# First chunk of a sparse-attention and MoE kernel: copies of the transposed exponentials ahead of the put-off weight operations

## The chip, the cores and the metric

The kernel runs on one core of one Trainium2 chip. The metric is the device time of one execution in microseconds (us); the time before is the median of three runs. A core has a matrix engine (TensorE, PE in the rows, its weight loads PEld), a vector engine (VectorE, DVE), a scalar engine (ScalarE, ACT), GpSimd (POOL) and SyncE (SP). Each engine takes its instructions in the order in which they are written for it, and they wait for each other by semaphores. DMAs are issued from the queues of SyncE, ScalarE and GpSimd; in the rows ACTq is ScalarE's queue where it issues one.

## What is computed

Block-sparse attention over 4 batches, 8 heads, 768 positions and 64 dimensions a head, and then a two-layer network with a gate on its output, cut here to what matters:

```python
scores = scale * np.matmul(q, k.transpose(0, 1, 3, 2))
scores = np.where(mask, scores, -1000000000.0)   # blocks of 32: the diagonal and its neighbours, the edges, 3 drawn ones a row
attn = np.exp(scores - np.max(scores, axis=-1, keepdims=True))
attn = attn / (np.sum(attn, axis=-1, keepdims=True) + 1e-09)
x = np.matmul(attn, v)                            # then laid out as 3072 tokens x 512
h = x @ w_in                                      # 512 -> 2048
g = h * (1.0 / (1.0 + np.exp(-1.702 * h)))
out = g @ w_out                                   # 2048 -> 512
```

## The kernel before

The tokens are worked in six chunks of 512. A chunk of the network has 16 steps (m, 0 to 15 in the first chunk), one for each slice of 128 of the inner dimension. In step m TensorE does twelve up-projection matmuls of slice m (L565 to L567, `up`) and twelve down-projection matmuls of slice m - 1 (L616, L617, L612, `down`). Each matrix is held as a high and a low part (`xhi`, `xlo`; the two halves of `win` and `wout`; `ghi`, `glo`), and each product is the sum of three of these matmuls. Between the two, ScalarE takes a tanh of the up-projection's bank (L573, `gate`), in steps before 13 also copies the bank to `wst` so that it comes free (L578), VectorE makes the gate (L580), ScalarE its high part (L585) and VectorE its low part (L593).

The attention of the next chunk runs between these matmuls, one item in two steps, by a plan that `plan` makes ahead of time. At the start of an even step TensorE computes an item's scores (L323) into banks 0 and 1 and, behind them, the values of the item before (L401) into bank 2. VectorE takes the rows' maximum (L340, L342) and normalises the item before (L417 to L427), and ScalarE does the exponentials (L354). At the start of the odd step behind it TensorE transposes the exponentials into banks 0 and 1 (L372) and the finished x of the item before into bank 2 (L434). ScalarE copies the two banks to `pt` (L378, two copies), and then makes x's high part (L441, `xhi`), from which VectorE makes the low part (L442, `xlo`). The next item's scores need banks 0 and 1 again, so they wait for the copies; the values need `pt` and bank 2, so they wait for the copies and for L442.

In the first chunk alone, `weights` also turns the 32 weight tiles from 64-bit words to two parts. A tile k is fetched by a DMA of 512 KB on ScalarE's queue (L467, `raw`). ScalarE takes the high word (L477, `a`), VectorE works three operations on it (L515, L517, L526), ScalarE casts the high part (L492) and, for a `wout` tile, issues its store to DRAM (L494, `ws`), and VectorE makes the low part (L485). Up-projection m needs `win` tile m, down-projection m needs `wout` tile m. `run(n0)`, `run(n1)` and `run(n2)` in `tick` let this generator take some steps. What it does on VectorE is written at once. What it does on ScalarE (the DMAs too) is put into the list `self.late`, and `self.flush()` writes the whole list. So the places where `tick` calls `flush` set where the weight operations stand among ScalarE's other instructions.

In `tick`, a step's first calls are the low part of the gate before (VectorE), `flush`, and `begin`, which writes what the plan has for the step's start. `begin` writes the matmuls at once and returns the rest in `after`: in an odd step the two copies and the pair L441 and L442, in an even step the maximum, the exponentials and the normalisation. `finish(after[:4])` writes them.

Of the kernel before, what the change touches and what calls it, by code (L numbers as in the profile page):

```python
# [39 lines left out]
QT = 4  # L40
# [14 lines left out]
class Kernel:  # L55
# [646 lines left out]
    def tick(self, m):  # L702

        n0, n1, n2 = 0, 0, 0
        if m < NF:
            heavy = any(part == self.scores for q in range(QT) for part, g in self.at.get(QT * m + q, ()))
            n0, n1, n2 = (2, 2, 4) if heavy else (2, 2, 2)

        def run(n):
            for _ in range(n):  # L710
                next(self.conv, None)

        def finish(todo):
            for f in todo:
                f()

        self.gate_lo(m - 1)
        self.flush()
        after = self.begin(QT * m)
        finish(after[:4])  # L720
        run(n0)
        finish(after[4:])
        self.up(m, range(0, 2))
        self.put_off = []
        finish(self.begin(QT * m + 1))
        put_off, self.put_off = self.put_off, None
        self.up(m, range(2, 4))
        after = self.begin(QT * m + 2)
        self.gate(m, lambda: (self.flush(), run(n1)))
        finish(put_off)  # L730
        finish(after[:3])
        self.down(m - LAG, 0)
        self.gate_hi(m)
        self.flush()
        finish(after[3:])
        finish(self.begin(QT * m + 3))
        self.down(m - LAG, 1)
        self.split(m + 1)
        self.stream(m + 3)
        run(n2)  # L740
# [315 lines left out]
```

## Time and profile before

| | |
|---|---|
| three runs, us | 744.56, 746.95, 746.97; median 746.95 |
| profiled execution, us | 741.64 |
| its span, us | 739.9 |
| busy, us (share of the span) | TensorE 719.3 (97%), weight loads 564.2 (76%), VectorE 449.8 (61%), ScalarE 388.4 (52%), GpSimd 63.3 (9%) |
| granted TensorE clock | 0.997 over the span |
| DMA | 122.97 MB, 166 GB/s over the span |

The shares of busy time are means over stages with different limits: the attention of the first units runs alone until about 75 us, the first chunk with the weights' conversion until about 197 us, and the other chunks behind it. A busy TensorE counts a matmul from its start to a modelled end, also where matmuls of one group wait for each other's banks. What a stage is worth is read from a table of stretches and from the timeline of that stage. In the table, steps are cut at the first up-projection matmul (L565) of each, so that a step's piece begins with its up-projection and ends with what the plan sets at the start of the step behind it: an even step's with the transposes, an odd step's with scores and values.

### The profile page before, as it was taken

What the parts mean: (1) busy time and instruction counts of PE and PEld (TensorE: products, weight loads), DVE (VectorE), ACT (ScalarE), POOL (GpSimd) and SP (SyncE); (2) the same over time, 40 slices, a digit from 0 to 9 for tenths busy, and PEclk for the clock granted to TensorE, in tenths of its full rate; (3) what the DMA queues carried; (4) which work ended last, traced back from release to release, by engine and by line L of the source; (5) the groups of instructions that cost most, each with busy time, mean ns of one, the idle gap of its engine ahead of it and who ended that gap; (6) DMA issues with size and microseconds to landing.
All of it is one profiled execution on the core that took longest, in us unless ns stands there. A gap on an engine that the chain in (4) does not pass through costs nothing.

```text
span 739.9 us, 18756 instructions
## 1 busy us (share of the span) xinstructions
PE 719.3 (97%) x7564; PEld 564.2 (76%) x7564; DVE 449.8 (61%) x839; ACT 388.4 (52%) x759; POOL 63.3 (9%) x105
## 2 busy tenths in 40 slices
PE   8899999998999999999999999999999999999996
PEld 5666777776777787777877787778878788888885
DVE  4595888788654445455444544554567877676552
ACT  4686666656554454445444454544334554445442
POOL 2245101011011111100111111100000000000000
PEclk9999999999999999999999999999999999999998
DMA  8997877768476576657565555631111301110532
GB/s 325 363 363 250 282 251 249 244 195 285 170 225 198 154 206 197 189 156 229 185 188 175 164 180 168 194 114 31 43 43 43 86 29 43 30 42 30 143 113 71
DMA packets 58776, 122.97 MB, mean 166 GB/s; under 512 B 7105, under 2 KB 24898, under 8 KB 58690
## 3 DMA queue, kind: packets, MB, share of 16 engines
q1 hardware_dynamic: 44978, 76.72, 34.0%
q0 software_dynamic: 6336, 23.43, 9.7%
q10 hardware_dynamic: 7376, 21.63, 8.6%
q8 instruction: 59, 0.97, 0.5%
q14 instruction: 27, 0.22, 0.1%
HBM read 111.26 MB, written 10.49 MB: 165 GB/s over the span
## 4 chain that ended last, share of the span: by engine, by line
PE 74%; DVE 11%; DMA 7%; ACT 5%; issue 2%; SPq 1%; ACTq 0%; POOL 0%; DVEq 0%
PE banks L612 10%; PE banks L616 10%; PE banks L617 9%; PE banks L825 9%; PE banks L565 6%; PE banks L566 5%; PE banks L567 5%; PE banks L401 5%; PE banks L372 5%; PE banks L323 5%; DMA raw<-in_moe_w_in_dram 2%; DMA vmid<-in_v_dram 2%; PE banks L333 1%; DVE g L580 1%; DVE a L517 1%
## 5 line engine op out<-in xcount | busy, mean ns | idle before, releaser
L616 PE MATMUL banks<-wout,ghi 128*128 128x512 f32 x384 | 151.5, 395 | 0.0
L617 PE MATMUL banks<-wout,ghi 128*128 128x512 f32 x384 | 149.9, 390 | 1.3 <-DVE wout L485 1.3
L354 ACT ACTIVATE ex<-banks,nm 128x256 f32<-128x256 f32 x176 | 69.0, 478 | 77.9 <-DVE rg L417 66.0
L612 PE MATMUL banks<-wout,glo 128*128 128x512 f32 x384 | 107.6, 394 | 1.2 <-DVE glo L593 1.2
L565 PE MATMUL banks<-xhi,win 128*128 128x512 f32 x256 | 105.0, 410 | 1.5 <-DVE g L580 1.1
L566 PE MATMUL banks<-xlo,win 128*128 128x512 f32 x256 | 100.3, 392 | 0.0
L567 PE MATMUL banks<-xhi,win 128*128 128x512 f32 x256 | 100.1, 391 | 0.0
L554 DVE TENSOR_TENSOR wout<-wst,wout 128x512 fp32r<-128x512 f32 x80 | 55.2, 690 | 68.6 <-ACT wout L553 68.0
L617 PEld LDWEIGHTS banks<-wout,ghi 128*128 128x128 f32 x384 | 72.2, 188 | 16.6 <-DVE wout L485 2.1
L616 PEld LDWEIGHTS banks<-wout,ghi 128*128 128x128 f32 x384 | 72.1, 188 | 15.9 <-ACT ghi L585 0.5
L573 ACT ACTIVATE g<-banks 128x512 f32<-128x512 f32 x64 | 38.5, 602 | 86.7 <-PE banks L567 86.7
L612 PEld LDWEIGHTS banks<-wout,glo 128*128 128x128 f32 x384 | 70.7, 188 | 17.3 <-DVE glo L593 2.8
L378 ACT COPY pt<-banks 128x512 f32<-128x512 f32 x112 | 60.9, 588 | 29.4 <-PE banks L372 27.0
L265 POOL DMA_INDIRECT vown<-in_v_dram,vidx x44 | 42.7, 970 | 380.2 <-PE banks L401 367.9
L585 ACT CAST ghi<-g 128x512 fp32r<-128x512 f32 x80 | 50.1, 626 | 45.4 <-DVE g L580 37.6
L580 DVE SCALAR_TENSOR_TENSOR g<-g,banks 128x512 f32<-128x512 f32 x51 | 35.0, 687 | 59.1 <-ACT g L573 58.7
L340 DVE TENSOR_REDUCE mx<-banks 128x4 f32<-128x1024 f32 x44 | 53.7, 1221 | 26.5 <-PE banks L323 24.5
L372 PEld LDWEIGHTS banks<-ident,ex 128*128 128x128 f32 x448 | 50.4, 140 | 18.1 <-ACT pt L378 6.7
L372 PE MATMUL banks<-ident,ex 128*128 128x128 f32 x448 | 61.0, 276 | 3.1 <-ACT pt L378 2.8
L565 PEld LDWEIGHTS banks<-xhi,win 128*128 128x128 f32 x256 | 48.1, 188 | 13.8 <-ACT wst L578 1.8
L401 PEld LDWEIGHTS banks<-vown,pt 128*32 128x32 f32 x1408 | 42.3, 109 | 18.4 <-issue 13.8
L567 PEld LDWEIGHTS banks<-xhi,win 128*128 128x128 f32 x256 | 48.1, 188 | 10.5
(111 smaller groups left out, 1098.9 us busy)
## 6 DMA issues: line engine op xcount, KB each, us to landing
wst<-ws SPq DMA_DIRECT2D x80, 256.0 KB, 2.7
kg<-in_kb_dram SPq DMA_DIRECT2D x126, 128.0 KB, 3.0
raw<-in_moe_w_in_dram ACTq DMA_DIRECT2D x16, 512.0 KB, 5.6
raw<-in_moe_w_out_dram ACTq DMA_DIRECT2D x16, 512.0 KB, 5.7
kg<-in_kb_dram SPq DMA_DIRECT2D x18, 384.0 KB, 5.3
vown<-in_vd_dram SPq DMA_DIRECT2D x8, 780.0 KB
vmid<-in_v_dram SPq DMA_DIRECT2D x22, 260.0 KB, 4.0
qt<-in_q_dram SPq DMA_DIRECT2D x22, 256.0 KB, 3.1
```

Of the source, the lines that this page charges most:

```text
L354: nc.scalar.activation(out=ex[:, cols], in_=sps[h][:, cols], func=AF.Exp, bias=un["nm"][:, c:c + 1], scale=SCALE)
L372: self.nc.tensor.transpose(ps[:, slot], g["ex"][h][:, k * P:(k + 1) * P], self.ident)
L378: self.nc.scalar.copy(out=pt, in_=ps)
L401: nc.tensor.matmul(sums[BLK * c:BLK * (c + 1), 2 * i + h], g["pt"][h][:, 2 * i + k, BLK * c:BLK * (c + 1)], src[:, at:at + DV], start=(k = ...
L554: self.nc.vector.tensor_tensor(out=t[:, DM:2 * DM], in0=w, in1=t[:, 0:DM].bitcast(F32), op=ALU.subtract)
L565: nc.tensor.matmul(h, wih[:, k], hi[:, k], start=(k == 0), stop=False)
L566: nc.tensor.matmul(h, wih[:, k], lo[:, k], start=False, stop=False)
L567: nc.tensor.matmul(h, wil[:, k], hi[:, k], start=False, stop=(k == NCT - 1))
L612: nc.tensor.matmul(o[n], glo[:, tk[n]], woh, start=False, stop=last)
L616: nc.tensor.matmul(o[n], ghi[:, tk[n]], woh, start=(f == 0), stop=False)
L617: nc.tensor.matmul(o[n], ghi[:, tk[n]], wol, start=False, stop=False)
L825: self.nc.tensor.matmul(bank, a[:, k], b[:, k], start=start and k + n == 0, stop=k == 1 and n == 2, skip_group_check=True)
```

## The change

```diff
--- before.py
+++ after.py
@@ -714,10 +714,13 @@
             for f in todo:
                 f()
 
+        turning = any(part == self.transposes for part, g in self.at.get(QT * m, ()))
         self.gate_lo(m - 1)
-        self.flush()
+        if not turning:
+            self.flush()
         after = self.begin(QT * m)
         finish(after[:4])
+        self.flush()
         run(n0)
         finish(after[4:])
         self.up(m, range(0, 2))
```

In a step whose plan begins with transposes, the first `flush` is left out, and the list is written behind `finish(after[:4])`. In the other steps the first `flush` stands as it did, and the second finds the list empty, since `begin` puts nothing into it. From step 16 on the list is always empty. The steps with transposes at their start and something in the list are 1, 3, 5, ... 15: eight places, all on ScalarE.

This is the piece of the order on ScalarE at the start of step 11 (`pt` takes the copies of the transposed exponentials; `a`, `raw` and `win` belong to the weight tiles; the tanh L573 is step 11's own):

```order
 L467 DMA raw<-in_moe_w_in_dram 128x1024
 L477 ACTIVATE a<-raw 128x512
+L378 COPY pt_130<-banks 128x512
+L378 COPY pt_131<-banks 128x512
+L441 CAST xhi_125<-banks 128x4x64
 L492 CAST win_1959<-a 128x512
 L467 DMA raw<-in_moe_w_out_dram 128x1024
 L477 ACTIVATE a<-raw 128x512
-L378 COPY pt_130<-banks 128x512
-L378 COPY pt_131<-banks 128x512
-L441 CAST xhi_125<-banks 128x4x64
 L573 ACTIVATE g<-banks 128x512
```

The copies and the cast of x have moved ahead of a weight cast, the issue of a transfer and an L477.

The same on ScalarE at the start of step 13:

```order
 L492 CAST wout_120<-a 128x512
 L494 DMA ws_95<-a 128x512
+L378 COPY pt_129<-banks 128x512
+L378 COPY pt_130<-banks 128x512
+L441 CAST xhi_125<-banks 128x4x64
 L467 DMA raw<-in_moe_w_in_dram 128x1024
 L477 ACTIVATE a<-raw 128x512
 L492 CAST win_1961<-a 128x512
-L378 COPY pt_129<-banks 128x512
-L378 COPY pt_130<-banks 128x512
-L441 CAST xhi_125<-banks 128x4x64
```

Here the three have moved ahead of the issue of a transfer, an L477 and a weight cast. The order of the three among themselves, and that of the weight operations among themselves, is as it was.

## Rows read from the trace of the kernel before

**Rows 1.** The page's chain of waits: shares of the span by engine.
```profile
PE 74%; DVE 11%; DMA 7%; ACT 5%; issue 2%; SPq 1%; ACTq 0%; POOL 0%; DVEq 0%
```

**Rows 2.** Stretches: A:B, length, busy us (instructions) of PE, PEld, DVE, ACT, POOL; clock, DMA.
```profile
87.17:196.92 109.75, 105.59 (x1084) 80.32 (x1079) 90.76 (x171) 69.97 (x138) 8.75 (x8) 1.00 0.72 235
196.92:739.87 542.95, 534.53 (x5146) 427.39 (x5140) 301.14 (x534) 260.54 (x513) 26.21 (x28) 1.00 0.43 128
```

**Rows 3.** Stretches: odd steps 3, 5, 7, 9, 11, and the sum of all seven.
```profile
93.75:102.05 8.30, 8.28 (x124) 5.99 (x122) 5.42 (x11) 5.08 (x11) 0.00 (x0) 1.00 0.52 165
109.34:117.09 7.75, 7.75 (x120) 5.87 (x120) 6.16 (x12) 5.77 (x11) 0.00 (x0) 1.00 0.80 259
123.91:132.52 8.61, 8.33 (x122) 6.01 (x121) 5.67 (x11) 5.32 (x11) 0.00 (x0) 1.00 0.58 189
139.82:148.14 8.32, 8.32 (x120) 6.22 (x120) 5.73 (x11) 5.67 (x11) 0.00 (x0) 1.00 0.88 270
155.37:164.53 9.16, 8.30 (x121) 6.01 (x121) 5.67 (x11) 5.33 (x11) 0.00 (x0) 1.00 0.46 153
...
sum 59.07, PE 56.82 PEld 41.73 DVE 41.51 ACT 37.02 POOL 0.92; mean PE 8.12 PEld 5.96 DVE 5.93 ACT 5.29 POOL 0.13
```

**Rows 4.** Stretches: even steps 2, 12, 14, and the sum of all seven.
```profile
87.17:93.75 6.58, 6.58 (x40) 5.57 (x35) 6.41 (x15) 4.54 (x10) 2.59 (x2) 1.00 0.85 296
...
164.53:171.83 7.30, 7.14 (x41) 5.48 (x35) 7.13 (x15) 4.87 (x11) 0.00 (x0) 1.00 0.97 298
180.75:188.91 8.16, 6.89 (x35) 5.50 (x35) 7.75 (x15) 5.22 (x11) 1.09 (x2) 1.00 0.87 292
sum 50.68, PE 48.77 PEld 38.59 DVE 49.24 ACT 32.95 POOL 7.83; mean PE 6.97 PEld 5.51 DVE 7.03 ACT 4.71 POOL 1.12
```

**Rows 5.** Waits, 87.17 to 196.92 us: us in total, times, longest.
```profile
DVE xlo L442 <- ACT xhi L441: 14.3, 6, 3.4
...
PE banks L617 <- DVE wout L485: 1.3, 1, 1.3
...
PE banks L565 <- DVE g L580: 1.1, 1, 1.1
```

**Rows 6.** ScalarE by line, the same stretch: count | busy, mean | idle before.
```profile
L477 ACT ACTIVATE a<-raw 128x512 f32<-128x512 f32 x23 | 15.7, 682 | 10.7 <-DMA raw<-in_moe_w_in_dram 7.1 <-DMA raw<-in_moe_w_out_dram 3.6
```

**Rows 7.** Timeline, ScalarE, step 11: start us, us, what, idle before.
```profile
156.85 0.68 ACT L477 ACTIVATE a<-raw 128x512 f32<-128x512 f32 x1
157.53 0.62 ACT L492 CAST win<-a 128x512 fp32r<-128x512 f32 x1
...
160.78 0.66 ACT L477 ACTIVATE a<-raw 128x512 f32<-128x512 f32 x1 [2.63 <-DMA raw<-in_moe_w_in_dram]
161.35 1.06 ACT L378 COPY pt<-banks 128x512 f32<-128x512 f32 x2
162.29 0.39 ACT L441 CAST xhi<-banks 128x256 fp32r<-128x256 f32 x1
```

**Rows 8.** Timeline, VectorE, steps 11 and 12.
```profile
158.64 0.69 DVE L593 TENSOR_TENSOR glo<-g,ghi 128x512 fp32r<-128x512 f32 x1
162.71 0.42 DVE L442 TENSOR_TENSOR xlo<-banks,xhi 128x256 fp32r<-128x256 f32 x1 [3.38 <-ACT xhi L441]
...
164.25 0.42 DVE L515 TENSOR_SCALAR a<-a 128x512 int32<-128x512 int32 x1
...
167.72 1.22 DVE L340 TENSOR_REDUCE mx<-banks 128x4 f32<-128x1024 f32 x1
```

**Rows 9.** Timeline, TensorE: scores at the start of step 12.
```profile
161.97 1.58 PE L323 MATMUL banks<-kg,qt 64*32 64x256 f32 x32 [0.86 <-ACT pt L378]
```

**Rows 10.** Timeline, ScalarE and its queue (ACTq), steps 13 and 14.
```profile
175.35 0.33 ACTq L467 DMA_DIRECT2D raw<-in_moe_w_out_dram  x1
175.52 0.61 ACT L492 CAST win<-a 128x512 fp32r<-128x512 f32 x1
...
178.48 0.72 ACT L477 ACTIVATE a<-raw 128x512 f32<-128x512 f32 x1 [0.61 <-DMA raw<-in_moe_w_in_dram]
```

## The prediction

> **What bounds the kernel now.** I read the chain of waits first. Over the whole run TensorE carries most of it, with VectorE, DMA and ScalarE behind [rows 1], so the first question is where those three have their shares. The table of stretches answers it: behind 196.92 us TensorE is busy 534.53 of 542.95 us, while the 109.75 us from 87.17 to 196.92 (steps 2 to 15 of the first chunk) leave it 4.16 us without work, and its busy time there also counts matmuls stretched by waits inside them [rows 2]. The change touches steps 1 to 15 alone, so this stretch is the place to look.
>
> Next I cut the stretch at the first up-projection matmul of each step. An odd step's piece, with the next item's scores and values at its end, lasts 7.75 us at best (step 5) and 9.16 at worst (step 11) [rows 3]. An even step's, with the transposes at its end, lasts 6.58 us at best (step 2), 8.16 at worst (step 14) and 50.68 together [rows 4]. The matmuls are the same in all steps of a kind, so I take the shortest as what TensorE needs. The excess is then: odd steps 3, 7, 9, 11: 0.55 + 0.86 + 0.57 + 1.41 = 3.39 us; odd steps 13 and 15 share the rest of the odd steps' 59.07 us: 59.07 - 7 x 7.75 - 3.39 = 1.43; even steps 50.68 - 7 x 6.58 = 4.62, of which step 14 has 8.16 - 6.58 = 1.58 and steps 4 to 12 share 3.04. Together 9.44 us of 109.75. That is all the change can win here.
>
> Then I asked the list of waits who makes them. VectorE idles 14.3 us, in six odd steps, until ScalarE's cast L441 releases the subtraction L442; two single waits of TensorE, 1.1 us for L580 and 1.3 us for L485, stand in step 14 [rows 5]. ScalarE in its turn idles 10.7 us before L477, all of it for weight transfers [rows 6]. So the order on ScalarE is late, that makes VectorE late, and that makes TensorE late.
>
> **The change, part by part.** Nothing is added or removed. On ScalarE alone, in eight steps (1, 3, ... 15), two copies of transposed exponentials (L378) and one cast of x (L441) go ahead of two to four put-off weight instructions. TensorE, VectorE, GpSimd and SyncE keep their orders.
>
> Step 11 in full. ScalarE runs L477 at 156.85, then the cast L492 at 157.53, then a second L477 that waits 2.63 us for its transfer until 160.78, and only then the two copies at 161.35 and the cast of x at 162.29 [rows 7]. The transposes were done before the step's first up-projection matmul at 155.37 [rows 3], so nothing but the order holds the copies back. After the change they take the place of L492: two copies from 157.53 to 158.6 (1.06) and the cast to 158.9 (it starts 0.94 after the copies and takes 0.39). L492 and the second L477 follow, and L477 is still free well before its transfer lands at 160.78.
> - VectorE: L442 came at 162.71, after 3.38 us of idling behind L593 at 158.64 [rows 8]. Now it can start at about 159.3. The next instruction that needs ScalarE's late work is L515, which reads what L477 leaves at 160.78 + 0.66 = 161.44; it ran at 164.25, so VectorE is 2.8 us ahead from there, and keeps a wait of about half a microsecond, for the transfer.
> - TensorE: the scores L323 started after 0.86 us of waiting for the copies, and took 1.58 us because the second copy came while they ran [rows 9]. With the copies done at 158.6 both go, and with x's subtraction done at 159.7 the values that write its bank do not wait either. The step falls to 7.75: 1.41 us.
> - The even step behind it: the maximum L340 ran at 167.72 [rows 8]. Its inputs are there earlier, so it moves by VectorE's 2.8 us while TensorE moves by 1.41. The exponentials then lead the transposes by 1.4 us more than before, and this covers step 12's 7.30 - 6.58 = 0.72 us.
>
> The sum over the steps:
> - Odd steps 3, 7, 9, 11: I carry step 11 over to the other three, where three or four weight instructions move in the same way. 3.39 us go, nothing stays.
> - Even steps 4 to 12: 3.04 us. VectorE's six idle stretches of 14.3 us shrink to the waits for transfers, which were 10.7 us of ScalarE's idling [rows 6] and now lie beside 7 x 1.33 = 9.3 us of copies and casts. I leave 0.3 us.
> - Steps 13 to 15: 1.43 + 1.58 = 3.01 us. Up-projection 14 starts after 1.1 us of waiting for L580, which is behind L442 on VectorE, and goes. The 1.3 us at L617 are for the weight half L485, which stands on VectorE behind step 14's maximum and normalisation, whose start TensorE itself sets. I leave 1.0 us.
> Gain 9.44 - 0.3 - 1.0 = 8.1, taken as 8.0 us.
>
> What it could cost: seven of the moved groups hold a weight transfer (L467), and its issue is now behind three more instructions. A transfer has no row in this place, so I bound it. At the top, its issue slips by the whole copies and cast, 1.33 us. At the bottom, nothing: in step 13 the transfer of the step after is issued at 175.35, while the weight cast, two copies, cast of x and tanh that stand ahead of it all start later, from 175.52 on [rows 10]; the queue passes them as soon as what they wait for is there. I take 0.2 us, nearer to that row. It hides wherever the reader comes late: step 11's is read one L477 behind the one that still waits at 160.78. Step 13's is read without slack (L477 at 178.48 waits 0.61 us for it [rows 10]); it stays inside the 1.0 us left above. The Trainium skill, page DMA: Bandwidth & Descriptors, section Rules for kernel authors, says to issue a DMA early, compute, and wait for it late, and so speaks against setting three instructions before each issue. By that rule a slip of 1.33 us would be paid at seven issues; the row of step 13 shows the issue passing such instructions, so the trace does not agree that it is paid here.
>
> VectorE does not become the bound: it has 90.76 us of work [rows 2] for the 100.3 us (7 x 14.33) that TensorE needs. The gain lasts, since TensorE is 98% busy behind 196.92 and starts all of it earlier.
>
> The profiled execution took 741.64 us (739.9 of span and 1.7 around it); the sum would bring it to 733.6. The three timed runs (744.56 to 746.97) lie above it, and nothing in the profile says where; I take the 8.0 us off their median: 746.95 - 8.0 = 739.0.
>
> **The rivals.**
> - Direct waits alone go. If VectorE, freed from L442, stands as long at L515 or L485 for ScalarE's moved weight operations, the exponentials come no earlier, and only the 3.39 us of the scores' waits are won: 743.6. For it: L515 and L485 both read ScalarE's results. Against it: in step 11 the moved L477 ends when its transfer lets it, in either order.
> - Transfers become the bound. With everything else earlier, L477 waits longer; 10.7 us of it [rows 6] are there already. Were half of the 3.04 and all but 0.5 of the 3.01 us to stay, the gain is 3.39 + 1.52 + 0.5 = 5.4: 741.5. For it: the DMA engines are busy 72% of the stretch [rows 2]. Against it: the issues hang on the same steps, so they come earlier too.
> - Slower: the weight chain is delayed. If the weight operations behind the copies, their transfers included, are what VectorE and then TensorE wait for last, each of seven steps adds 1.33 us, 9.3 in all, less the 3.39: 5.9 us slower, 752.9. It decides from the point where the transfer's issue really slips by the copies and its reader has no slack; the trace shows that slack missing in step 13 alone. The Trainium skill's rule on early issue, in DMA: Bandwidth & Descriptors, Rules for kernel authors, would lead here.
> - No change: the steps get shorter, but the lead is lost to a wait behind 196.92, for instance on stored weights read back; 746.95. Against it stands TensorE's 98% there.
>
> **How the numbers follow.** A measurement of this kernel tells about 0.5%, 3.7 us, from no change. Forecast (gain 5.6 to 9.4): 0.60. Transfers: 0.17. Direct waits alone: 0.13. No change 0.05, slower 0.05. The range takes in the forecast, the transfers and the direct waits: from 735.2 (the whole 9.44 us off the middle of the runs and their spread) to 743.8. The forecast's own range is 737.5 to 741.3. Faster: 0.60 + 0.17 + nearly half of 0.13 = 0.83. Within 0.5%: 0.12. Slower: 0.05.
>
> **What would show it.** The stretch between the first up-projection matmuls of steps 2 and 16 falls from 109.75 to about 101.6 us, odd steps near 7.75 and even ones near 6.6. L442's waits for L441 fall from 14.3 us to under 4; ScalarE's waits for transfers stay or grow; no scores wait for L378; at L617 a wait for L485 may stay. I am wrong if VectorE's idling only changes its place to L515 or L485, if even steps keep 7.3 us, or if step 13 or 14 waits longer for a weight tile than before.

## The result and the profile after

The change took the median from 745.75 us (four runs of the kernel before, 743.33 to 746.97) to 734.75 (four runs, 733.50 to 735.92): a ratio of 0.9856, interval 0.9822 to 0.989. The forecast was 739.0 and its range began at 735.2, so the time lies 0.45 us below the range. The profiled execution took 734.98 us, with a span of 733.2.

In all tables below, the stretch runs from the first up-projection matmul of step 2 to that of step 16, and "opening" is what lies before step 0's. The columns of the next fences are those of [rows 2]. First the two stretches of the kernel after:

```profile
89.32:190.24 100.92, 100.40 (x1085) 79.85 (x1079) 89.04 (x168) 68.89 (x137) 7.49 (x8) 1.00 0.79 256
190.24:733.20 542.96, 534.49 (x5146) 427.29 (x5140) 301.21 (x534) 260.76 (x513) 26.22 (x28) 1.00 0.43 128
```

The stretch fell from 109.75 us [rows 2] to 100.92, by 8.83, and all behind it stayed at 542.96: the gain lasts. The chain of waits, which had VectorE at 11% and ScalarE at 5 [rows 1], by engine after:

```profile
PE 82%; DMA 7%; DVE 6%; ACT 3%; issue 1%; ACTq 0%; DVEq 0%
```

TensorE gained the shares that the two lost. The odd step 11 and the sum of the seven odd steps, after:

```profile
153.10:160.82 7.72, 7.72 (x124) 5.85 (x122) 4.83 (x9) 3.89 (x9) 0.00 (x0) 1.00 0.56 218
...
sum 54.04, PE 54.04 PEld 40.96 DVE 44.88 ACT 35.98 POOL 0.00; mean PE 7.72 PEld 5.85 DVE 6.41 ACT 5.14 POOL 0.00
```

The even steps 12 and 14, after:

```profile
160.82:167.40 6.58, 6.58 (x40) 5.56 (x35) 6.33 (x13) 4.52 (x10) 0.00 (x0) 1.00 0.90 277
175.12:182.52 7.40, 6.88 (x40) 5.49 (x35) 7.16 (x15) 5.03 (x11) 1.87 (x2) 1.00 0.96 296
```

All seven odd steps take 7.72 us and six of the seven even ones 6.58; the scatter of [rows 3, 4] is gone but for step 14, 0.82 us above the others. ScalarE and VectorE by line in the stretch, after (columns as in [rows 6]):

```profile
L477 ACT ACTIVATE a<-raw 128x512 f32<-128x512 f32 x23 | 15.6, 678 | 15.7 <-DMA raw<-in_moe_w_in_dram 9.0 <-DMA raw<-in_moe_w_out_dram 4.2 <-DMA kg<-in_kb_dram 1.4
L515 DVE TENSOR_SCALAR a<-a 128x512 int32<-128x512 int32 x23 | 9.8, 424 | 7.9 <-ACT a L477 7.6
...
L442 DVE TENSOR_TENSOR xlo<-banks,xhi 128x256 fp32r<-128x256 f32 x7 | 2.9, 419 | 0.0
```

VectorE's 14.3 us of idling before L442 [rows 5] are gone. The idling moved to two places where TensorE doesn't feel it: before L515 on VectorE, and before L477 on ScalarE, which idles 5.0 us longer than before [rows 6]; the view puts 13.2 of these 15.7 us down to weight transfers, and all 10.7 before. Step 11 shows how. ScalarE and its queue, after (columns as in [rows 7]):

```profile
151.46 0.33 ACTq L467 DMA_DIRECT2D raw<-in_moe_w_in_dram  x1
151.93 0.69 ACT L477 ACTIVATE a<-raw 128x512 f32<-128x512 f32 x1
152.73 1.08 ACT L378 COPY pt<-banks 128x512 f32<-128x512 f32 x2
153.39 0.33 ACTq L467 DMA_DIRECT2D raw<-in_moe_w_out_dram  x1
153.69 0.39 ACT L441 CAST xhi<-banks 128x256 fp32r<-128x256 f32 x1
153.95 0.65 ACT L492 CAST win<-a 128x512 fp32r<-128x512 f32 x1
158.09 0.66 ACT L477 ACTIVATE a<-raw 128x512 f32<-128x512 f32 x1 [3.49 <-DMA raw<-in_moe_w_in_dram]
...
167.93 0.34 ACTq L467 DMA_DIRECT2D raw<-in_moe_w_in_dram  x1
...
173.60 0.69 ACT L477 ACTIVATE a<-raw 128x512 f32<-128x512 f32 x1 [1.17 <-DMA raw<-in_moe_w_in_dram]
```

VectorE, after:

```profile
150.68 0.69 DVE L580 SCALAR_TENSOR_TENSOR g<-g,wst 128x512 f32<-128x512 f32 x1
...
154.33 0.42 DVE L442 TENSOR_TENSOR xlo<-banks,xhi 128x256 fp32r<-128x256 f32 x1
...
158.78 0.43 DVE L515 TENSOR_SCALAR a<-a 128x512 int32<-128x512 int32 x1 [2.84 <-ACT a L477]
...
162.26 1.22 DVE L340 TENSOR_REDUCE mx<-banks 128x4 f32<-128x1024 f32 x1
```

TensorE at the start of step 12 and in step 14, after:

```profile
158.75 1.09 PE L323 MATMUL banks<-kg,qt 64*32 64x256 f32 x32
...
178.88 0.50 PE L617 MATMUL banks<-wout,ghi 128*128 128x512 f32 x1 [0.52 <-DVE wout L485]
```

ScalarE still stands 3.49 us for the late transfer at step 11, but nothing that TensorE needs is behind it. L442 runs at 154.33, 1.2 us after the step's first matmul at 153.10; it was 7.3 us after [rows 3, 8]. The scores take 1.09 us with no wait, where they waited 0.86 and took 1.58 [rows 9]. Step 14 keeps the wait for L485 that the prediction left standing, 0.5 for 1.3 us [rows 5].

Now compare with the same two places of the kernel before, the gate L580 of step 10 and the transfer's issue behind it:

```profile
155.61 0.69 DVE L580 SCALAR_TENSOR_TENSOR g<-g,wst 128x512 f32<-128x512 f32 x1
156.39 0.33 ACTq L467 DMA_DIRECT2D raw<-in_moe_w_in_dram  x1
```

Before, L580 came 0.24 us after step 11's first matmul (155.37), after the change 2.42 us ahead of it (153.10); the transfer is issued 0.78 us behind L580 in both. So the late order carried itself on as far as the issue: ScalarE late, VectorE late, gate late, transfer issued late. Much less of it came back to ScalarE: the issue moved 2.66 us forward within step 11, but the L477 that reads this transfer only 0.42 us (4.99 us after the step's first matmul, 5.41 before [rows 7]). It starts 6.63 us behind the issue now, 4.39 before, and why the transfer takes longer is not shown. In steps 3, 7 and 9 the late L477 moved forward by 0.8, 1.5 and 2.0 us. Of the issues the forecast had only that they "hang on the same steps"; that they also come earlier within a step, by 2.7 us, it did not see.

### The profile page after: what moved, and what is told of

The parts are those of the page before. It is cut to its first block, busy times and chain, and to the rows that moved or that the text cites. A ratio compares the mean times of both kernels' runs of the same rounds, so it can differ in the third digit from the quotient of the medians.

```text
span 733.2 us, 18760 instructions
## 1 busy us (share of the span) xinstructions
PE 714.7 (97%) x7564; PEld 563.2 (77%) x7564; DVE 449.8 (61%) x839; ACT 388.4 (53%) x759; POOL 62.0 (8%) x105
## 4 chain that ended last, share of the span: by engine, by line
PE 82%; DMA 7%; DVE 6%; ACT 3%; issue 1%; ACTq 0%; DVEq 0%
PE banks L612 11%; PE banks L616 11%; PE banks L617 10%; PE banks L828 10%; PE banks L565 7%; PE banks L566 7%; PE banks L567 7%; PE banks L401 6%; PE banks L372 5%; PE banks L323 5%; DMA vown<-in_v_dram,vidx 3%; DMA raw<-in_moe_w_in_dram 2%; PE banks L333 1%; DMA raw<-in_moe_w_out_dram 1%; PE banks L434 1%; DVE gs L751 1%
## 5 line engine op out<-in xcount | busy, mean ns | idle before, releaser
L617 PE MATMUL banks<-wout,ghi 128*128 128x512 f32 x384 | 149.8, 390 | 0.5 <-DVE wout L485 0.5
L573 ACT ACTIVATE g<-banks 128x512 f32<-128x512 f32 x64 | 38.4, 599 | 87.5 <-PE banks L567 87.4
L617 PEld LDWEIGHTS banks<-wout,ghi 128*128 128x128 f32 x384 | 72.1, 188 | 15.4 <-DVE wout L485 0.9
L580 DVE SCALAR_TENSOR_TENSOR g<-g,banks 128x512 f32<-128x512 f32 x51 | 35.0, 687 | 59.0 <-ACT g L573 58.7
```

Source lines behind the costliest of these rows:

```text
L617: nc.tensor.matmul(o[n], ghi[:, tk[n]], wol, start=False, stop=False)
```

## The experiments

Four comparisons were made, each with its own runs of the kernel before. The profile of every run was cut at the same matmuls (us; the time is that of the profiled execution):

| kernel | opening | stretch | time |
|---|---|---|---|
| before; again (three) | 75.25; 74.56, 76.67, 75.87 | 109.75; 109.79, 109.47, 112.57 | 741.64; 741.26, 742.86, 745.38 |
| after; again (two) | 77.39; 76.89, 75.92 | 100.92; 100.41, 100.49 | 734.98; 733.86, 733.09 |
| copies alone ahead | 76.16 | 110.45 | 744.15 |
| cast alone ahead; again | 78.65; 75.81 | 103.74; 100.82 | 738.99; 733.77 |
| before, small transfers | 75.90 | 101.33 | 733.77 |
| after, small transfers | 75.56 | 100.10 | 732.46 |
| after, issues first | 77.69 | 100.10 | 734.32 |
| after, weight half earlier | 75.29 | 100.51 | 732.47 |

**Both kernels again** (no edit). First question: the first pair's openings, of unchanged code, differed by 2.14 us. Is that the change's, or scatter?

> The kernel before, once more, with its profile. Theory A (the change acts in steps 2 to 15 alone, and the three microseconds by which it beat the forecast are in how far the profiled execution of before lies below its timed runs): the time lies near 745, the first up-projection matmul comes later than the 75.25 us of the first profile (near 77), and the stretch from the first up-projection matmul of step 2 to that of step 16 is 109 to 112 us. Theory B (the change also saves time outside that stretch): the opening is again near 75.3 us, the stretch near 109.8, and the missing microseconds are behind step 16.

> The changed kernel, once more. Theory A: stretch of steps 2 to 15 again 100.9 us within 0.5, since no transfer reaches TensorE any more; opening free to differ by one or two microseconds; ratio to before 0.984 to 0.989. Theory B: the stretch differs between executions by as much as the total does.

The opening of before came out at 74.56, the one of after at 76.89. Theory A's time near 745 and opening near 77 did not come, and neither did theory B's saving behind step 16: from there on all 14 profiles take 542.9 to 543.1 us, so profiled executions differ in the opening and the stretch alone. Over all 14 profiles the opening lies between 74.56 and 78.65, the ranges of old and new order overlap (74.56 to 76.67, 75.29 to 78.65), and the code there is the same; I take it as scatter. The stretches repeated to 0.5 us. Timed, after against before was 736.15 to 743.97, ratio 0.9895 (0.9868 to 0.9922).

**Which of the moved instructions counts.** Here and below the edits are to the changed kernel, in the first chunk's turning steps (those that begin with transposes; the other steps stay as they are), and cut to the lines that matter, unless the text says otherwise. Copies alone ahead of the weight operations, the cast and L442 behind them:

```diff
-        finish(after[:4])
-        self.flush()
+            finish(after[:2])
+            self.flush()
+            finish(after[2:4])
```

> Only the two copies go ahead of the put-off weight operations; the cast of x stays behind them. Theory A (what counts is that VectorE no longer stands at x's low part behind an L477 that waits for a transfer; the copies alone win the scores' waits): VectorE still idles 10 us and more before L442, even steps keep about 7.2 us, odd steps lose most of their 3.4 us unless the values wait for L442; gain 2 to 4 us, ratio 0.994 to 0.998. Rival (the copies are what counts, since TensorE waits for them): as good as the whole change, gain 8 us and more, ratio below 0.989.

Measured: 741.64 to 743.97, ratio 0.9964 (0.9942 to 0.9986), as expected; but L442 idled 7.7 us and not over 10, and of the even steps 4 to 12 only 10 and 12 stayed near 7.2 (7.15 and 7.09). The profiled execution fell into a hole in step 15, 13.07 us long. ScalarE and TensorE by time there, and then the whole step and three microseconds of it as stretches:

```profile
188.64 0.66 ACT L477 ACTIVATE a<-raw 128x512 f32<-128x512 f32 x1 [3.96 <-DMA raw<-in_moe_w_out_dram]
...
190.83 0.49 PE L616 MATMUL banks<-wout,ghi 128*128 128x512 f32 x1 [2.37 <-ACT wout L492]
```

```profile
185.46:198.53 13.07, 9.86 (x124) 6.94 (x122) 6.77 (x11) 4.67 (x9) 0.00 (x0) 0.87 0.21 72
...
194.00:197.00 3.00, 3.00 (x31) 2.09 (x37) 1.80 (x4) 1.14 (x2) 0.00 (x0) 0.66 0.10 36
```

A transfer for which ScalarE waited 3.96 us made a down-projection matmul wait 2.37, and behind the gap the granted clock fell to 0.66 of full speed while TensorE was busy all the time. This transfer was issued 0.36 us after step 14's first matmul (0.42 in the kernel before) and read 10.8 us later (7.4 before); why it took so long is not shown. Without the 5.35 us by which this step exceeds 7.72, the stretch would be 105.1, so the table's 110.45 is not what the copies alone leave; the timed gain is 2.3 us. Moving the copies without the cast leaves VectorE late, and the issues with it: in step 11 the transfer is issued 1.01 us after the first matmul, as before (1.02).

The cast and L442 alone ahead, the copies behind:

```diff
-        finish(after[:4])
-        self.flush()
+            finish(after[2:4])
+            self.flush()
+            finish(after[:2])
```

> Only the cast of x goes ahead; the two copies stay behind the put-off weight operations. Theory A: VectorE's idling before L442 goes, even steps fall to near 6.6 us and steps 13 to 15 lose most of their excess; the odd steps keep waits of the scores for the copies of 2 to 4 us in all; gain 4.5 to 7 us, ratio 0.990 to 0.994. Rival (the copies count): gain under 2 us.

> Only the cast of x ahead, once more: its timed runs were as fast as the whole change, though its profiled stretch was 3 us longer. Theory A (the profiled execution was an unlucky one, where three transfers landed late ahead of the copies): the stretch is shorter this time, 101 to 103 us, and steps with an excess stand where ScalarE waits for a transfer; ratio within 0.002 of the whole change's in the same session or up to 0.004 above it. Rival (the copies' place is worth its 3 us in every execution): stretch 103.3 to 104.2 again, ratio 0.003 to 0.005 above the whole change's.

Measured: 734.76 to 743.97, ratio 0.988 (0.9854 to 0.9907), and in another comparison 733.64 to 743.2, 0.9863 (0.9836 to 0.989): all of the change's gain (0.9895 and 0.9891 in the same comparisons), more than was expected of the first. Its first profile, of the longest of its six runs, shows what the copies' place still costs. The stretch and step 9:

```profile
90.61:194.35 103.74, 102.33 (x1085) 80.46 (x1078) 89.33 (x168) 68.72 (x137) 7.85 (x8) 1.00 0.78 250
140.78:149.63 8.85, 8.46 (x123) 6.17 (x121) 6.86 (x13) 5.89 (x13) 0.00 (x0) 1.00 0.87 267
```

and ScalarE in step 9:

```profile
145.18 0.66 ACT L477 ACTIVATE a<-raw 128x512 f32<-128x512 f32 x1 [2.79 <-DMA raw<-in_moe_w_in_dram]
...
146.25 1.05 ACT L378 COPY pt<-banks 128x512 f32<-128x512 f32 x2
```

Where a transfer is late, the copies are late with it and the step takes 8.85 instead of 7.72; three of seven odd steps did so here, and in the second profile two, by 0.2 and 0.3 us. L442 idled 0.0 us in both. So the link that matters is VectorE's, through the cast; with VectorE early the copies come in time in most steps, wherever they stand.

**Taking the cause away instead.** If transfers that land late are what the old order put ahead of the copies, the old order costs nothing with transfers that are never late. In the kernel before, and in the changed one, the weight transfers from the ninth on fetch 64 bytes of each partition instead of 4 KB (into three fixed buffers in turn), so that most weights are stale:

```diff
-                nc.scalar.dma_start(out=raw, in_=self.w64[i][f])
+                n = 2 * DM if k < 8 else 16
+                nc.scalar.dma_start(out=raw[:, 0:n], in_=self.w64[i][f][:, 0:n])
```

> The kernel before, in which the weight transfers from the ninth on bring 64 bytes a partition instead of 4 KB, so most weights are left as an earlier transfer had them; the instructions and their order are those of before. Theory A (the copies and the cast of x were late because a weight operation ahead of them stood waiting for its transfer): ScalarE's waits for these transfers fall from 10.7 us to under 2, VectorE's idling before L442 from 14.3 to under 6, and the stretch of steps 2 to 15 from 109.8 to 101.5 to 104 us, though no instruction has moved. Rival (it is the number of instructions ahead of the copies that makes them late, whatever they wait for): the stretch stays above 106.5 us.

> The changed kernel with the same small transfers from the ninth on. Theory A: nothing is left to win but step 14's rest; stretch 100.2 to 100.7 us, so the change is worth 1 to 3.5 us here in place of 9. Rival: the change is still worth 6 us or more over the kernel before with small transfers.

Measured: 733.97 and 733.63 to 742.16; ratios 0.9887 (0.9869 to 0.9904) and 0.9885 (0.9866 to 0.9904). The old order with small transfers, its stretch, and L477 (line 485 there) and L442 by line:

```profile
87.83:189.16 101.33, 100.43 (x1085) 79.86 (x1079) 90.23 (x171) 69.59 (x138) 8.99 (x8) 1.00 0.47 142
```

```profile
L485 ACT ACTIVATE a<-rawn 128x512 f32<-128x512 f32 x23 | 15.8, 686 | 0.5 <-ACT wout L500 0.5
...
L442 DVE TENSOR_TENSOR xlo<-banks,xhi 128x256 fp32r<-128x256 f32 x7 | 3.0, 424 | 6.6 <-ACT xhi L441 6.5
```

With no instruction moved, the stretch falls to 101.33. L442 still idles 6.6 us (under 6 were expected), for the plain work of the weight operations ahead of the cast, and this is hidden: it is the wait for transfers inside it that TensorE pays. (The DMA engines are busy 47% there, 72% before, so other transfers gain too; that the order alone does it, the changed kernel shows.) On top of small transfers the change is worth 1.2 us (101.33 to 100.10), all of it in step 14 (7.81 to 6.59), which the timed runs do not tell from nothing.

**Does the issue slip?** In the changed kernel, the put-off transfers are issued ahead of the copies, and the rest of the list stays behind them (`issue` writes the list's L467 alone):

```diff
         if not turning:
             self.flush()
+        else:
+            self.issue()
         after = self.begin(QT * m)
```

> The changed kernel, but in the steps that begin with transposes the put-off issues of weight transfers go first, ahead of the copies, and the other put-off operations behind them, as in the change. Theory A (the queue passes the copies, a transfer is issued no later for standing behind them): ScalarE's waits for transfers stay within 3 us of the changed kernel's 14 to 16, the stretch stays within 0.5 us of its 100.4 to 100.9. Rival (each issue slips by the copies and the cast, 1.3 us): the waits for transfers fall by 5 us or more, and step 14 or another one gets shorter.

Measured: 734.04 to 742.16, ratio 0.9896 (0.9876 to 0.9916). Its stretch, step 14, and the issues in steps 11 and 13:

```profile
89.61:189.71 100.10, 100.10 (x1084) 79.93 (x1079) 89.85 (x168) 69.61 (x137) 7.94 (x8) 1.00 0.79 257
175.41:182.00 6.59, 6.59 (x41) 5.58 (x35) 6.32 (x14) 4.89 (x10) 1.87 (x2) 1.00 0.96 302
```

```profile
152.95 0.33 ACTq L467 DMA_DIRECT2D raw<-in_moe_w_out_dram  x1
...
167.69 0.39 ACTq L467 DMA_DIRECT2D raw<-in_moe_w_in_dram  x1
```

Steps 11 and 13 begin at 153.40 and 167.69 here, at 153.10 and 167.40 in the changed kernel. From the step's start the issue comes at -0.45 and 0.00 us here, at +0.29 and +0.53 there: behind the copies it slips by 0.74 and 0.53 us. L477 (line 479 here) idles 11.9 us in the stretch, 15.7 there (16.1 and 14.4 in its other profiles): 2.5 to 4.2 us less, between what the two theories expected. Only step 14 pays: 6.59 here, 7.40, 6.89 and 6.97 us in the three profiles of the changed kernel. This is the shortest stretch of any version with whole transfers, 7 x (7.72 + 6.58) = 100.1, though by a single profile; the timed runs don't tell it from the change.

**Step 14's weight half.** L485 was brought ahead of step 14's maximum by one step of the generator:

```diff
+            if m == 13:
+                n2 = 3
+            if m == 14:
+                n0 = 1
```

> The changed kernel with one instruction moved: VectorE makes the low half of the weight tile for down-projection 13 (L485) ahead of step 14's maximum and normalisation instead of behind them. Theory A: step 14 falls from 6.9 to 7.4 us to 6.6, the stretch to 100.1 to 100.4 us; too little for the timed runs to tell from the change. Rival (the half is late for its transfer): step 14 stays above 6.8 us.

Measured: 733.98 to 742.16, ratio 0.9885 (0.9868 to 0.9903). Steps 14 and 15:

```profile
173.01:179.60 6.59, 6.59 (x42) 5.58 (x35) 6.45 (x14) 4.08 (x10) 1.87 (x2) 1.00 0.97 272
179.60:187.73 8.13, 8.01 (x124) 5.77 (x122) 6.12 (x11) 4.67 (x9) 0.00 (x0) 1.00 0.35 136
```

Step 14 falls to 6.59 and step 15 rises by 0.4, where the weight load of an L617 waits 0.5 us for the next tile's L485; the stretch of 100.51 is a little above what was expected. So a weight half is late in one step or the other.

**The level.** The medians fell by 11.0 us in the first comparison and by 7.8 in the second, where 8.0 were forecast, so both kernels were profiled again.

> The kernel before, a third profile. Theory A (what scatters between executions is the opening, 74.6 to 78.7 us in the ten profiles so far, and the two profiles of before, at 75.25 and 74.56, lay at its low end): time minus opening is again 666.4 to 667.0 us, with a stretch of 109.3 to 111 us; a time near 744 goes with an opening near 77. Rival (the stretch itself scatters in before): a time near 745 with an opening near 75 and a stretch of 112 us or more.

> The kernel before, a fourth profile; the same expectations as for the third.

> The changed kernel, a third profile and timed beside the one above. Theory A: stretch 100.1 to 101, the steps before 14 at 6.6 and 7.7 us to a tenth; ratio 0.986 to 0.990, since 9.1 us of stretch are 1.2% of 743.

Measured: 742.86 and 745.38 us of before in single runs, 734.04 to 743.2 of after, ratio 0.9891 (0.9853 to 0.9929). The third profile of before was much as theory A has it, the fourth was the rival's case: its opening took 75.87 us and its stretch 112.57, most of the excess in one step. ScalarE and TensorE in that step 9:

```profile
147.28 0.66 ACT L477 ACTIVATE a<-raw 128x512 f32<-128x512 f32 x1 [4.05 <-DMA raw<-in_moe_w_in_dram]
...
148.98 2.34 PE L323 MATMUL banks<-kg,qt 64*32 64x256 f32 x32 [2.55 <-ACT pt L378]
```

and the stretches of the whole step and of four pieces, the last already in step 10:

```profile
140.68:153.14 12.46, 9.91 (x120) 7.18 (x120) 7.24 (x14) 5.74 (x12) 0.00 (x0) 0.87 0.57 188
```

```profile
146.40:149.00 2.60, 0.05 (x2) 0.02 (x1) 0.00 (x0) 1.72 (x4) 0.00 (x0) 1.00 0.37 134
149.00:151.00 2.00, 2.00 (x32) 1.09 (x32) 1.24 (x3) 2.00 (x5) 0.00 (x0) 0.71 0.86 246
151.00:153.20 2.20, 2.20 (x72) 1.78 (x65) 2.20 (x5) 0.38 (x2) 0.00 (x0) 0.50 0.06 19
153.20:155.00 1.80, 1.80 (x10) 1.50 (x9) 1.77 (x4) 1.57 (x3) 1.41 (x2) 0.98 0.56 109
```

A transfer 4.05 us late held the copies, the scores waited 2.55 us, and behind that gap they took 2.34 us where they take 1.09, at a granted clock that fell to 0.50. The step cost 12.46 - 7.72 = 4.7 us: 2.55 of wait and, as an estimate from the clock of the two pieces, 2.00 x 0.29 + 2.20 x 0.50 = 1.7 of lost clock. None of the changed kernel's three profiles has such a step.

## Why the prediction was right and wrong

**Right: the mechanism and its size.** The forecast took 8.0 us off the stretch of steps 2 to 15; the pair of profiles lost 8.83. Against the prediction's terms: odd steps 3 to 11 and the even steps 4 to 12 lost all their excess (0.3 us of the even ones was to stay, 0.0 did). Of steps 13 to 15, 1.0 us was to stay and 0.82 did, in the step and at the wait that were named. The odd steps' need was read as 7.75 us from the best one and is 7.72, which gives 0.2 more over seven. What it said a profile would show came in each point: L442 without waits, scores without waits, longer waits for transfers on ScalarE. The wait at L515 grew from 0.6 to 7.6 us, which was named as a sign of being wrong, and yet even steps fell to 6.58: VectorE's idling changed its place, but to one where the maximum is not late. L442 was forecast at 159.3, 3.9 us after step 11's first matmul, and came 1.2 after it; the wait at L515 there was forecast at half a microsecond and is 2.84: the size of this shift was misjudged, and it cost nothing. Another sign came on ScalarE, whose L477 at the end of step 13 waits 1.17 us for its weight tile and waited 0.61 [rows 10]; TensorE's wait for L485 behind it still fell, from 1.3 to 0.5. One reading was wrong without harm to the sum: the wait for L580 ends at 180.75, where step 14 begins, so its 1.1 us are in step 13's piece. The rival of direct waits alone is refuted by these even steps, that of the transfers by the stretch, and the slower one by the sign.

**Wrong: the level it was taken from.** The step that failed reads: "I take the 8.0 us off their median: 746.95 - 8.0 = 739.0." The other comparisons put the kernel before at 743.97, 742.16 and 743.2; of its 44 timed runs (740.61 to 751.83, median 743.4) 31 lie below the lowest of the three that were shown. 743.4 - 8.0 = 735.4, and all 16 timed runs of after have their median at 734.9: by this count some 3.6 us of the miss of 4.25 are the level, and some 0.5 the gain. The four runs of the first comparison alone would split it otherwise, 1.2 for the level (745.75) and 3.0 for a gain of 11.0; the stretch (8.83 us) and the other two comparisons (7.8 and 9.2) speak for the first count. Why the runs of before that were shown lay high stays open; the three later comparisons ran on three different chips, and after's medians (734.75, 736.15, 734.04) did not move with those of before. The profiled execution at 741.64 stood 5 us below the median of the three runs, a sign that runs of this kernel scatter that far; 8.0 us off it gave 733.6, only some 1.1 us from the measured median, in part by luck, since openings differ by up to 4 us. The range used the scatter of three runs only, and "the whole 9.44 us off the middle of the runs and their spread" could not reach below 735.2.

What scatters is seen in the profiles only: the opening (74.56 to 78.65) and, in the kernel before, single steps with a transfer that comes late. In the opening of after's first profile, TensorE waits 2 us for gathered values between 30 and 50 us (us in all, times, longest), and its clock is lower from 40 to 50. The wait of after, and the stretch of before and of after:

```profile
PEld banks L401 <- DMA vown<-in_v_dram,vidx: 2.0, 1, 2.0
```

```profile
40.00:50.00 10.00, 9.96 (x173) 6.88 (x172) 9.53 (x23) 8.56 (x16) 5.01 (x12) 1.00 0.98 391
```

```profile
40.00:50.00 10.00, 9.45 (x170) 5.81 (x171) 7.15 (x17) 6.02 (x11) 4.48 (x11) 0.83 0.95 361
```

No term of the sum held the second kind. The four profiles of before have a mean stretch of 110.4 us, the three of after 100.6, so 9.8 us, and 9.1 without the fourth. That the change takes such steps away is not shown by one case in four against none in three, and timed runs of after still reach 740.02. How often timed runs meet such a step can't be read from them, since only profiled executions can be cut; what part of a timed run's scatter is which stays open.

**Undersized: the issue's slip.** It was taken as 0.2 us, nearer to the row in which the queue passed five instructions [rows 10], between bounds of 0 and 1.33; in steps 11 and 13 it is 0.74 and 0.53. Most of it hides, as was said. The place that has no slack was named rightly, and pays 0.3 to 0.8 us in step 14 (three profiles against one). The Trainium skill's rule of issuing a DMA early (DMA: Bandwidth & Descriptors, section Rules for kernel authors) is so borne out in its direction by the version with the issues first, whose step 14 takes 6.59 us. It was no reason against the change, since the change also brings the list's issues as a whole forward.

## What to carry to other kernels

Before an instruction that waits for a transfer is written into an engine's stream, look at what stands behind it: work for another engine that doesn't need the transfer goes ahead, and, by one profile here, the transfer's issue ahead of both. If the held engine also sets when the next transfer is issued, a late transfer makes the next issue late, and it pays to look for the one link in this chain that can be moved (here a cast of 0.39 us). When a profiled execution and the timed runs lie 5 us apart, a forecast in absolute time needs a range that holds both levels; the difference from the profile was known far better than the level.

## What was not expected of the hardware

After 2.6 us without matmuls (146.40 to 149.00 in the fourth profile of before), TensorE's granted clock went to 0.71 and then 0.50, 1.2 of 2.4 GHz, while TensorE was busy throughout, and was back at 0.98 for the stretch behind 153.20. So a step with a wait of 2.55 us took 4.7 longer. The hole in step 15 of the kernel with the copies alone (a wait of 2.37 us, then 0.66) and the opening of after (a wait of 2.0, and 0.83 from 40 to 50 us) show the same on a smaller scale.
